# Four or eight of the sixteen d_ff tiles of the input stage as seven products of quarters in blocks 4, 5, 7 and 8, with the attention of those blocks in one PSUM tile and some squares on GpSimd

## The chip, the cores and the metric

The kernel runs on one core of one Trainium2 chip. The metric is device time in microseconds (us) of one execution, from inputs in device memory to the output in device memory; the median of a few executions is given. A profiled execution also has a span, from its first to its last instruction.

## The reference

Attention in chunks of 64 tokens, followed by a feed-forward layer with a squared ReLU:

```python
B, H, S, D = 8, 8, 576, 64            # q, k, v: float32
scores = matmul(q_c, k_c.T) / sqrt(D) # q_c, k_c, v_c: chunks of 64 tokens
attn = softmax(scores)
x = matmul(attn, v_c)                 # -> [B * S, H * D] = [4608, 512]
h = maximum(x @ w_in, 0)              # w_in [512, 2048]
out = (h * h) @ w_out                 # w_out [2048, 512], float32
```

## The kernel before

The 4608 tokens are cut into 18 groups of 256 (`GT`) and the groups, two by two, into nine blocks of 512 tokens, block 0 to block 8 (line 41). Matmuls take bf16 operands and accumulate in float32. d_model = 512 is four row tiles of 128 (`n_dt`), d_ff = 2048 sixteen column tiles (`n_ft`).

**The input stage of a block** is `ffn_in` (line 455). For each of the 16 d_ff tiles `ft`, in `FT_ORDER` 8 to 15 and then 0 to 7, it takes one of four PSUM banks `ps_ffn`, issues four matmuls of 512 columns (line 480: 128 rows of `w_in_bf` stationary, `xT` moving), has ScalarE write the ReLU to `rl` in SBUF (line 471; three buffers), and squares `rl` into `gT`, on VectorE (line 475) or, for tiles 10, 14 and 3, on ScalarE (line 473). From block 3 on `rl` is float32, in blocks 0 to 2 bf16. A `yield` after each tile ends a step, or slot.

**The output stage** is `ffn_out` (line 498; block 0 uses `ffn_out_by_ft`). It multiplies `gT` (512 tokens by 2048) by `w_out` with Winograd's form of Strassen's method: halves of the tokens, of d_ff and of d_model give seven products instead of eight, each 16 matmuls of 256 columns (line 533) in two steps. VectorE makes five differences of quarters of `gT` (line 513, printed as line 493, since the helper `add` records all of them there; `d5`, `d2`, `d1`, `d6`, `d7`, in tiles `w_st`), and combines the products (`w`, `c21`, `s`, `c12`, `c22`, line 493 too). ScalarE copies `n1`, `n2`, `c11` out of PSUM (lines 580, 589, 616).

**Attention runs beside it, one block ahead.** While block j is multiplied, the groups of block j+1 go through `scores` (SC: 32 matmuls into a PSUM tile `ps_att`, exponential on ScalarE, lines 374 and 385), `values` (AV: for each of two token tiles 16 matmuls of 65 columns into a `ps_att` tile, line 401, a reciprocal and a product on VectorE, lines 408 and 409) and `transpose_x` (XT: a DMA transpose from SyncE, line 422, into `xT`). `ps_att` has two buffers of two PSUM banks, so that one tile is filled while another is read. For block j+2 the queries and keys are loaded, cast (CQ, CK; on ScalarE from group 8 on, lines 333 and 340) and transposed by DMA (TD, line 351).

**What sets the order.** The schedule is manual: each engine executes its instructions in the order in which the program issues them. The loop at line 711 writes, for each block, a plan: which of SC, AV, XT, CQ, CK, TD follows which slot (line 745 on: SC after slots 4, AV after 7 and 11, XT after 10 and 14 in blocks 4, 5 and 7 where the line at 750 does not change them), one load per slot in `go_slots`, all on SyncE's queue, and the stores of the block before from slot 20 on (`LATE_STORES`, line 451). The last block has no attention beside it. GpSimd casts the weights and the queries and keys of groups below 8, and issues early and last stores; between 84.7 us and 270.9 us of the span it executes nothing.

## Time and profile before

| | |
|---|---|
| median of three runs | 280.62 us (279.8 to 282.45) |
| the profiled execution: its time | 281.17 us |
| the profiled execution: its span | 279.4 us |
| granted TensorE clock, mean | 0.997 |
| busy: PE, VectorE (DVE), ScalarE (ACT), GpSimd (POOL) | 269.2, 186.5, 160.5, 35.8 us |

The profiled execution's time is 1.8 us above its span and 0.55 us above the median. Times below are us from the start of the span; PE is TensorE's matmuls, PEld its weight loads, and L480 is line 480 of the kernel before. In the groups of instructions a row has the busy time and the mean duration (ns) of one instruction after the count; instructions of one engine overlap a little at their ends, so that a row of them takes less than the sum of their durations. In the chain of waits, pieces of work are listed in order of time, each the one that the next waited for: start, duration, what it was.

The stages of blocks 4 to 8, by the times at which the chain changes from L480 to L533 and back:

| block | input stage with attention | output stage |
|---|---|---|
| 4 | 138.01 to 153.79 | to 166.02 |
| 5 | 166.02 to 181.57 | to 193.80 |
| 6 | 193.80 to 209.61 | to 222.06 |
| 7 | 222.06 to 237.61 | to 249.84 |
| 8 (no attention) | 249.84 to 263.65 | to 275.89 |

### The profile page before, as it was taken

What the parts mean: (1) busy time and instruction counts of PE and PEld (TensorE: products, weight loads), DVE (VectorE), ACT (ScalarE), POOL (GpSimd) and SP (SyncE); (2) the same over time, 40 slices, a digit from 0 to 9 for tenths busy, and PEclk for the clock granted to TensorE, in tenths of its full rate; (3) what the DMA queues carried; (4) which work ended last, traced back from release to release, by engine and by line L of the source; (5) the groups of instructions that cost most, each with busy time, mean ns of one, the idle gap of its engine ahead of it and who ended that gap; (6) DMA issues with size and microseconds to landing.
All of it is one profiled execution on the core that took longest, in us unless ns stands there. A gap on an engine that the chain in (4) does not pass through costs nothing.

```text
span 279.4 us, 7179 instructions
## 1 busy us (share of the span) xinstructions
PE 269.2 (96%) x2960; PEld 176.2 (63%) x2963; DVE 186.5 (67%) x304; ACT 160.5 (57%) x269; POOL 35.8 (13%) x62
## 2 busy tenths in 40 slices
PE   6789999989999999999999999999999999999994
PEld 4544455878774487448744874487448744874584
DVE  1446414998943595579549954995579649955793
ACT  2537615885348862877197719762877197218710
POOL 2037844240171000000000000000000000000012
PEclk9999999999999999999999999999999999999998
DMA  7999999989999999979999999979699964141003
GB/s 236 220 345 358 364 332 240 326 212 194 255 207 244 238 213 191 258 183 198 218 245 260 187 184 298 191 158 185 196 238 208 212 199 40 39 109 44 0 21 131
DMA packets 144384, 57.09 MB, mean 204 GB/s; under 512 B 110624, under 2 KB 141600, under 8 KB 144352
## 3 DMA queue, kind: packets, MB, share of 16 engines
q1 hardware_dynamic: 143296, 53.62, 83.8%
q0 software_dynamic: 912, 2.88, 2.8%
q8 instruction: 23, 0.38, 0.6%
q10 hardware_dynamic: 144, 0.13, 0.1%
q14 instruction: 9, 0.07, 0.1%
HBM read 36.70 MB, written 9.44 MB: 165 GB/s over the span
## 4 chain that ended last, share of the span: by engine, by line
PE 80%; DVE 6%; SPq 4%; ACT 2%; DMA 2%; issue 2%; POOL 0%; DVEq 0%; ACTq 0%
PE ps_ffn L480 39%; PE ps_ffn L533 32%; PE ps_ffn L626 5%; SPq L236 3%; DMA w_st<-in_moe_w_in_dram 2%; DVE x L409 2%; DVE gT L475 2%; DVE w_st L493 2%; ACT rl L471 2%; PE ps_att L401 2%; PE ps_att L374 1%; ACT e L385 1%; SPq L227 1%; PE ps_att L428 1%; PE ps_att L190 1%
## 5 line engine op out<-in xcount | busy, mean ns | idle before, releaser
L480 PE MATMUL ps_ffn<-xT,w_in_bf 128*128 128x512 bf16 (+1 forms) x640 | 130.0, 358 | 0.7 <-POOL w_in_bf L165 0.7
L475 DVE TENSOR_TENSOR gT<-rl 128x512 bf16<-128x512 f32 (+2 forms) x132 | 74.2, 593 | 61.4 <-ACT rl L471 60.7
L471 ACT ACTIVATE rl<-ps_ffn 128x512 f32<-128x512 f32 (+2 forms) x160 | 85.7, 554 | 26.9 <-PE ps_ffn L480 23.3
L480 PEld LDWEIGHTS <-w_in_bf 128*128 128x128 bf16 x640 | 60.5, 98 | 58.2 <-POOL w_in_bf L165 2.2
L533 PEld LDWEIGHTS <-w_st 128*128 128x128 bf16 x640 | 62.0, 98 | 8.2 <-DVE w_st L493 0.9
L493 DVE TENSOR_TENSOR w_st<-gT 128x2048 bf16<-128x2048 bf16 x40 | 47.3, 1217 | 0.2
L533 PE MATMUL ps_ffn<-w_out_bf,w_st 128*128 128x256 bf16 x384 | 45.1, 273 | 0.1
L533 PE MATMUL ps_ffn<-w_sum,w_st 128*128 128x256 bf16 x256 | 29.6, 273 | 0.0
L616 ACT COPY o_sb<-ps_ffn 128x512 f32<-128x512 f32 (+1 forms) x8 | 4.5, 559 | 40.3 <-PE ps_ffn L533 40.3
L533 PEld LDWEIGHTS <-gT 128*128 128x128 bf16 x256 | 24.8, 98 | 4.4 <-DVE gT L475 0.2
L568 POOL DMA_DIRECT2D out_dram<-o_sb x4 | 2.2, 553 | 186.2 <-DVE o_sb L493 186.2
L409 DVE TENSOR_TENSOR x<-ps_att,rec 128x512 bf16<-128x512 f32 x32 | 22.1, 691 | 1.1
L385 ACT ACTIVATE e<-ps_att 128x1024 bf16<-128x1024 f32 x16 | 15.8, 1022 | 4.8 <-PE ps_att L374 4.8
L473 ACT ACTIVATE gT<-rl 128x512 bf16<-128x512 f32 (+2 forms) x28 | 16.8, 599 | 0.9
L533 PE MATMUL ps_ffn<-w_out_bf,gT 128*128 128x256 bf16 x128 | 15.3, 273 | 0.0
L533 PE MATMUL ps_ffn<-w_sum,gT 128*128 128x256 bf16 x128 | 15.3, 273 | 0.0
L626 PE MATMUL ps_ffn<-w_out_bf,gT 128*128 128x512 bf16 x61 | 14.2, 379 | 0.3 <-issue 0.2
L165 POOL CAST w_in_bf<-w_st 128x1024 bf16<-128x1024 f32 (+1 forms) x9 | 9.0, 1001 | 17.9 <-DMA w_st<-in_moe_w_in_dram 17.9
L340 ACT CAST qkb<-k_sb 128x1024 bf16<-128x1024 f32 x10 | 10.5, 1047 | 1.2 <-DMA k_sb<-in_k_dram 1.2
L333 ACT CAST qkb<-q_sb 128x1024 bf16<-128x1024 f32 x10 | 10.4, 1044 | 0.0
L626 PEld LDWEIGHTS <-gT 128*128 128x128 bf16 x64 | 6.0, 98 | 7.0
L401 PEld LDWEIGHTS <-e 64*64 64x64 bf16 x512 | 5.8, 107 | 6.3 <-DVE x L409 2.1
(63 smaller groups left out, 157.1 us busy)
## 6 DMA issues: line engine op xcount, KB each, us to landing
q_sb<-in_q_dram SPq DMA_DIRECT2D x16, 512.0 KB, 6.2
k_sb<-in_k_dram SPq DMA_DIRECT2D x24, 256.0 KB, 5.8
out_dram<-o_sb SPq DMA_DIRECT2D x20, 256.0 KB, 3.7
w_st<-in_moe_w_in_dram SPq DMA_DIRECT2D x8, 512.0 KB, 6.8
w_st<-in_moe_w_out_dram SPq DMA_DIRECT2D x8, 512.0 KB, 6.1
ve_sb<-in_v_dram SPq DMA_DIRECT2D x28, 128.0 KB, 3.5
vo_sb<-in_v_dram SPq DMA_DIRECT2D x21, 128.0 KB, 3.0
out_dram<-o_sb POOLq DMA_DIRECT2D x9, 256.0 KB, 5.5
```

The source lines that it names most:

```text
L333: copy(out=qkb[:, 0].rearrange("p (i h d) -> p i h d", i=2, h=H), in_=qk[g][0].rearrange("p t h d -> p (t h d)").rearrange("p (h i d) -> p ...
L340: copy(out=state["qkb", g][:, 1], in_=qk[g][1].rearrange("p t h d -> p (t h d)"))
L385: nc.scalar.activation(out=e_out, in_=s_in, func=AF.Exp, scale=scale)
L401: nc.tensor.matmul(out=ps[64 * p:64 * p + 64, a, hp * (D + 1):(hp + 1) * (D + 1)], lhsT=e[64 * c:64 * c + 64, a, hp, t, :], rhs=vb[64 * c: ...
L409: nc.vector.tensor_tensor(out=x[:, t].rearrange("p h a d -> p a h d"), in0=o[:, :, :, 0:D], in1=rec.to_broadcast([128, 2, n_hp, D]), op=AL ...
L471: nc.scalar.activation(out=rl[:, 0:n], in_=h[:, 0:n], func=AF.Relu)
L473: nc.scalar.activation(out=gT[:, ft, c:c + n], in_=rl[:, 0:n], func=AF.Square)
L475: nc.vector.tensor_tensor(out=gT[:, ft, c:c + n], in0=rl[:, 0:n], in1=rl[:, 0:n], op=ALU.mult)
L480: nc.tensor.matmul(out=h[:, 0:n], lhsT=w_in_bf[:, dt, ft * 128:(ft + 1) * 128], rhs=xT[:, c // 128:(c + n) // 128, dt, :], start=(dt == 0) ...
L493: engine.tensor_tensor(out=out, in0=in0, in1=in1, op=op)
L533: nc.tensor.matmul(out=outs[t], lhsT=a[:, i, t * 128:(t + 1) * 128], rhs=b[:, i, :], start=(first and i == 0 and (last or t == 0)), stop=( ...
L626: nc.tensor.matmul(out=o_ps[tt], lhsT=gT[:, ft, tt * 128:(tt + 1) * 128], rhs=w_out_bf[:, ft, :], start=(ft == 0), stop=(ft == n_ft - 1))
```

## The change

**Units.** `ffn_in_units` replaces `ffn_in` in blocks 4, 5, 7 (one unit: d_ff tiles 12 to 15) and 8 (two units: 12 to 15 and 4 to 7). A unit computes its four d_ff tiles by seven products instead of eight, with quarters of two d_ff tiles, two d_model tiles and 256 tokens: each product is four matmuls of 256 columns, 28 in all, in place of 16 of 512 columns. A unit has seven steps, `a` (or `b`), placed between the other tiles by `ORDER_U1` and `ORDER_U2`. The products go to the two halves of one `ps_att` tile. A unit has 2 copies (`n1`, `n2`) and a ReLU (`c11`) on ScalarE, on VectorE four combinations with PSUM (`nm`, `c21`, `s`, `c22`) and three fused ReLU-squares (`relu_squared`) from SBUF, on GpSimd one difference (`c12`) and one square. The names `n1`, `nm`, `n2` have one buffer each.

**Weights and tokens.** Five differences of quarters of `w_in` per set of tiles are made on GpSimd: for tiles 12 to 15 issued in block 3, for 4 to 7 in block 7 (slot 20), into query and key buffers. `x_sums`, three VectorE sums or differences of `xT`, are issued before the last product of the output stage of the block before.

**Attention.** In those blocks one `ps_att` tile belongs to the unit and the other serves all of SC and AV, so each scores or values tile writes where the one before was read. The slots are 5, 11, 13, 14 (SC, first AV tile, second AV tile, XT) for the first group and 9, 15, 17, 19 for the second; CQ, CK, TD and the late stores come three slots later.

**Squares.** Of the remaining tiles, 10, 0, 3, 5 are squared on GpSimd, 9, 1, 4 on ScalarE and the rest (8, 11, 2, 6, 7) on VectorE; in block 8, 8, 10, 1, 2 on GpSimd and 9, 11, 0, 3 on ScalarE. `rl` has four buffers instead of three, queries and keys four instead of five.

```diff
--- before.py
+++ after.py
@@ -58,7 +58,7 @@
...
-    in_pool = ctx.enter_context(tc.tile_pool(name="qk", bufs=5))
+    in_pool = ctx.enter_context(tc.tile_pool(name="qk", bufs=4))
...
@@ -74,6 +74,7 @@
...
+    w_dif = w_pool.tile([128, 5, n_dt // 2, 256], BF16, name="w_dif")
...
@@ -363,7 +364,7 @@
...
-        ps = ps_att.tile([128, 1024], FP32, name="ps_att")
+        ps = state.get("ps_att") or ps_att.tile([128, 1024], FP32, name="ps_att")
         for hp in range(n_hp):
             for t in range(2):
                 for a in range(2):
@@ -392,7 +393,8 @@
             state["x", g] = att_pool.tile([128, 2, n_hp, 2, D], BF16, name="x", bufs=3)
         x = state["x", g]
         for t in tiles:
-            ps = ps_att.tile([128, 2, 512], FP32, name="ps_att")
+            ps = state.get("ps_att") or ps_att.tile([128, 1024], FP32, name="ps_att")
+            ps = ps.rearrange("p (a c) -> p a c", a=2)
...
@@ -435,6 +437,12 @@
     C, CQ, CK, TD = cast_qk, cast_q, cast_k, transpose_qk_dma
     SC, AV, XT = scores, values, transpose_x
 
+    def AV0(g):
+        values(g, (0,))
+
+    def AV1(g):
+        values(g, (1,))
+
...
@@ -449,8 +457,144 @@
 
     gTs = {}
     LATE_STORES = {j: 26 if j == 2 else 20 for j in range(2, len(blocks) - 1)}
+    UNITS = {4: (12,), 5: (12,), 7: (12,), 8: (12, 4)}
+    for j in UNITS:
+        if j in LATE_STORES:
+            LATE_STORES[j] += 3
     late = []
     FT_ORDER = [*range(n_ft // 2, n_ft), *range(n_ft // 2)]
+
+    def rl_tile_fp32():
+        return ffn_pool.tile([128, 512], FP32, name="rl", bufs=4)
+
+    difs = {}
+
+    def quarter(f0, i, kk):
+        c = (f0 + 2 * i) * 128
+        return w_in_bf[:, 2 * kk:2 * kk + 2, c:c + 256]
+
+    def w_differences(f0, out):
+        pairs = (((0, 0), (0, 1)), ((1, 1), (1, 0)), ((0, 0), (1, 1)), ((1, 0), (0, 0)),
+                 ((0, 1), (1, 1)))
+        difs[f0] = out
+        for d, (x, y) in zip(out, pairs):
+            add(nc.gpsimd, d, quarter(f0, *x), quarter(f0, *y), ALU.subtract)
+
+    def w_differences_again(_):
+        q_sb = in_pool.tile([128, 2, H, D], FP32, name="q_sb").bitcast(BF16).rearrange(
+            "p t h d -> p (t h d)").rearrange("p (n a f) -> p n a f", n=4, a=2)
+        k_sb = in_pool.tile([128, 2, H, D], FP32, name="k_sb").bitcast(BF16).rearrange(
+            "p t h d -> p (t h d)").rearrange("p (n a f) -> p n a f", n=4, a=2)
+        w_differences(UNITS[8][1], [q_sb[:, n] for n in range(4)] + [k_sb[:, 0]])
+
+    def x_sums(j):
+        xT = xTs[j]
+        st = [wst_pool.tile([128, 1024], FP32, name="w_st").bitcast(BF16) for _ in range(2)]
+        by_dt = st[0][:, 0:1024].rearrange("p (t a q) -> p t a q", t=4, a=2)
+        by_t = st[0][:, 1024:2048].rearrange("p (t a q) -> p t a q", t=2, a=4)
+        cross = st[1][:, 0:512].rearrange("p (t a q) -> p t a q", t=2, a=2)
+        add(nc.vector, by_dt, xT[:, :, 0:2], xT[:, :, 2:4])
+        add(nc.vector, cross, xT[:, 0:2, 0:2], xT[:, 2:4, 2:4], ALU.subtract)
+        add(nc.vector, by_t, xT[:, 0:2], xT[:, 2:4])
+        return by_dt, by_t, cross
+
+    def unit(j, f0, ps):
+        gT, xT = gTs[j], xTs[j]
+        by_dt, by_t, cross = state["x_sums"]
+        n, m = ps[:, 0:512], ps[:, 512:1024]
+        dif = difs[f0]
+
+        def product(out, a, b, first):
+            for f in range(2):
+                for d in range(2):
+                    nc.tensor.matmul(
+                        out=out[:, 256 * f:256 * f + 256],
+                        lhsT=a[:, d, 128 * f:128 * f + 128],
+                        rhs=b[:, :, d, :],
+                        start=(first and f == 0 and d == 0), stop=(d == 1),
+                        skip_group_check=True)
+
+        def kept(name):
+            return ffn_pool.tile([128, 512], FP32, name=name)
+
+        def place_of(i, jj):
+            return gT[:, f0 + 2 * i:f0 + 2 * i + 2, 256 * jj:256 * jj + 256]
+
+        def both(x):
+            return x.rearrange("p (f q) -> p f q", f=2)
+
+        def relu_squared(x, i, jj):
+            nc.vector.scalar_tensor_tensor(
+                out=place_of(i, jj), in0=both(x), scalar=0.0, in1=both(x),
+                op0=ALU.max, op1=ALU.mult)
+
+        product(n, quarter(f0, 1, 1), by_dt[:, 0:2], True)
+        n1 = kept("n1")
+        nc.scalar.copy(out=n1, in_=n)
+        yield
+        product(m, quarter(f0, 0, 0), by_dt[:, 2:4], True)
+        w = kept("nm")
+        add(nc.vector, w, m, n1)
+        yield
+        product(n, dif[0], xT[:, 2:4, 2:4], False)
+        n2 = kept("n2")
+        nc.scalar.copy(out=n2, in_=n)
+        yield
+        product(m, dif[1], xT[:, 0:2, 0:2], False)
+        c21 = rl_tile_fp32()
+        add(nc.vector, c21, w, m, ALU.subtract)
+        c12 = rl_tile_fp32()
+        add(nc.gpsimd, c12, w, n2, ALU.subtract)
+        relu_squared(c21, 1, 0)
+        yield
+        product(n, dif[2], cross, False)
+        s = kept("n1")
+        add(nc.vector, s, n, n2, ALU.subtract)
+        relu_squared(c12, 0, 1)
+        yield
+        product(m, dif[3], by_t[:, :, 0:2], False)
+        c22 = rl_tile_fp32()
+        add(nc.vector, c22, m, s)
+        relu_squared(c22, 1, 1)
+        yield
+        product(n, dif[4], by_t[:, :, 2:4], False)
+        c11 = rl_tile_fp32()
+        nc.scalar.activation(out=c11, in_=n, func=AF.Relu)
+        add(nc.gpsimd, place_of(0, 0), both(c11), both(c11), ALU.mult)
+        yield
+
+    ORDER_U1 = (8, 9, 10, "a", 11, "a", 0, "a", 1, "a", 2, "a", 3, "a", 4, "a", 5, 6, 7)
+    ORDER_U2 = (8, 9, "a", 10, "a", 11, "a", "b", "a", 0, "b", "a", "b", "a", 1, "b", "a", "b",
+                2, "b", "b", 3)
+    SQUARE_BY = {1: {9: "A", 1: "A", 4: "A", 10: "P", 0: "P", 3: "P", 5: "P"},
+                 2: {9: "A", 11: "A", 0: "A", 3: "A", 8: "P", 10: "P", 1: "P", 2: "P"}}
+
+    def ffn_in_units(j):
+        gT, xT = gTs.setdefault(j, ffn_pool.tile([128, n_ft, BT], BF16, name="gT")), xTs[j]
+        ps = [ps_att.tile([128, 1024], FP32, name="ps_att") for _ in range(2)]
+        state["ps_att"] = ps[1]
+        units = UNITS[j]
+        if len(units) == 1:
+            todo, order = {"a": unit(j, units[0], ps[0])}, ORDER_U1
+        else:
+            todo, order = {"a": unit(j, units[0], ps[0]), "b": unit(j, units[1], ps[1])}, ORDER_U2
+        for ft in order:
+            if ft in todo:
+                next(todo[ft])
+                yield
+                continue
+            h = ps_ffn.tile([128, 512], FP32, name="ps_ffn")
+            for dt in range(n_dt):
+                ffn_in_step(h, xT, 0, BT, ft, dt)
+            rl = rl_tile_fp32()
+            nc.scalar.activation(out=rl, in_=h, func=AF.Relu)
+            by = SQUARE_BY[len(units)].get(ft)
+            if by == "A":
+                nc.scalar.activation(out=gT[:, ft], in_=rl, func=AF.Square)
+            else:
+                add(nc.gpsimd if by == "P" else nc.vector, gT[:, ft], rl, rl, ALU.mult)
+            yield
+        state.pop("ps_att")
 
     def ffn_in(j, parts, begun={}):
         if j not in gTs:
@@ -464,10 +608,10 @@
                 ffn_in_step(h, xT, c, n, ft, dt)
             if j < 3:
                 if n == 512 or u % 2 == 0:
-                    rl_tile = ffn_pool.tile([128, 512], FP32, name="rl", bufs=3).bitcast(BF16)
+                    rl_tile = ffn_pool.tile([128, 512], FP32, name="rl", bufs=4).bitcast(BF16)
                 rl = rl_tile[:, u % 2 * 512:] if n < 512 else rl_tile
             else:
-                rl = ffn_pool.tile([128, 512], FP32, name="rl", bufs=3)
+                rl = rl_tile_fp32()
             nc.scalar.activation(out=rl[:, 0:n], in_=h[:, 0:n], func=AF.Relu)
             if (n == 512 and ft in SQUARES_ON_ACT) or (n < 512 and ft in (12, 3)):
                 nc.scalar.activation(out=gT[:, ft, c:c + n], in_=rl[:, 0:n], func=AF.Square)
@@ -609,6 +753,8 @@
         for ps, cols, t in parts("m"):
             add(nc.vector, c22[:, cols], ps, s[:, cols])
             store(nc.gpsimd, c22, 1, HD, t)
+        if j + 1 in UNITS:
+            state["x_sums"] = x_sums(j + 1)
         yield from product("n", d7, b21_p_b22, False)
         c11 = o_tile()
         for ps, cols, t in parts("n"):
@@ -752,18 +898,31 @@
                 loads = itertools.chain(*map(v_pieces, nxt), loads)
                 slots = {SC: (8, 10), AV: (12, 15), XT: (15, 18), C: (20, 23), TD: (22, 25)}
                 go_slots = [*range(16), *range(25, 36)]
+            late_by = 0
+            if j in UNITS:
+                late_by = 3
+                go_slots = range(35)
+                for i, g in enumerate(nxt):
+                    for slot, f in zip(((5, 11, 13, 14), (9, 15, 17, 19))[i], (SC, AV0, AV1, XT)):
+                        at(slot, f, g)
+                nxt = []
+            if j == 3:
+                at(2, lambda _: w_differences(UNITS[4][0], [w_dif[:, n] for n in range(5)]), None)
+            if j == 7:
+                at(20, w_differences_again, None)
             for f in (SC, AV, XT):
                 for i, g in enumerate(nxt):
                     at(slots[f][i], f, g)
             if j > 2 and far and is_whole(far[0]):
                 for slot, f, i in ((16, CQ, 0), (18, CK, 0), (18, TD, 0), (18, CQ, 1),
                                    (19, CK, 1), (19, TD, 1)):
-                    at(slot, f, far[i])
+                    at(slot + late_by, f, far[i])
             else:
                 for f in (C, TD):
                     for i, g in enumerate(far):
-                        at(slots[f][i], f, g)
-            phases = [ffn_in(j, [(0, BT, FT_ORDER)]), ffn_out(j)]
+                        at(slots[f][i] + late_by, f, g)
+            phases = [ffn_in_units(j) if j in UNITS else ffn_in(j, [(0, BT, FT_ORDER)]),
+                      ffn_out(j)]
         slot = 0
         for phase in phases:
             for _ in phase:
```

## Prediction

> **What bounds the kernel now.** I read the page's busy shares first, then the chain of waits in order of time, then the groups of instructions by shape, and last the timelines of VectorE, ScalarE and GpSimd inside block 4. TensorE is the bound, and not only in the mean:
>
> ```profile
> PE 269.2 (96%) x2960; PEld 176.2 (63%) x2963; DVE 186.5 (67%) x304; ACT 160.5 (57%) x269; POOL 35.8 (13%) x62
> ```
>
> The chain of waits shows where. From block 4 on it runs on PE almost without a break:
>
> ```profile
> 138.01 4.32 PE ps_ffn L480 x20
> 142.33 0.38 PE ps_att L374 x32
> ...
> 146.28 3.56 PE ps_ffn L480 x16
> 149.84 0.39 PE ps_att L401 x27
> 150.23 3.56 PE ps_ffn L480 x16
> 153.79 12.23 PE ps_ffn L533 x112
> ...
> 249.84 13.81 PE ps_ffn L480 x64
> 263.65 12.24 PE ps_ffn L533 x112
> ```
>
> The last two lines give the two prices that count: 13.81 / 64 = 0.2158 us for a matmul of 512 columns, 12.23 / 112 = 0.1092 for one of 256. The groups by shape give the other engines' prices:
>
> ```profile
> L475 DVE TENSOR_TENSOR gT<-rl 128x512 bf16<-128x512 f32 x78 | 51.2, 687 | 41.6 <-ACT rl L471 41.1
> L409 DVE TENSOR_TENSOR x<-ps_att,rec 128x512 bf16<-128x512 f32 x32 | 22.1, 691 | 1.1
> L385 ACT ACTIVATE e<-ps_att 128x1024 bf16<-128x1024 f32 x16 | 15.8, 1022 | 4.8 <-PE ps_att L374 4.8
> L165 POOL CAST w_in_bf<-w_st 128x512 bf16<-128x512 f32 x2 | 1.2, 613 | 14.7 <-DMA w_st<-in_moe_w_in_dram 14.7
> ```
>
> Back to back, VectorE's instructions of 512 follow each other by 0.605 (two in 1.29), ScalarE's ReLUs by 0.50, its exponentials by 0.92; a dependent square starts 0.63 after its ReLU. ScalarE starts 0.25 after a tile's last matmul slot (tile begun 137.85, ReLU at 138.97). VectorE or ScalarE releases PE in 0.04 to 0.05.
>
> The timelines hold one more fact, from block 0, the only stretch with the weight casts: a VectorE square, 0.42 alone, takes 1.07 when it starts inside a GpSimd cast, and ends just after it.
>
> ```profile
> 23.46 0.42 DVE L475 TENSOR_TENSOR gT<-rl 128x512 bf16<-128x512 bf16 x1 [1.49 <-ACT rl L471]
> 25.25 1.07 DVE L475 TENSOR_TENSOR gT<-rl 128x512 bf16<-128x512 bf16 x1 [0.19 <-ACT rl L471]
> 25.00 1.04 POOL L165 CAST w_in_bf<-w_st 128x1024 bf16<-128x1024 f32 x1 [0.22 <-DMA w_st<-in_moe_w_in_dram]
> ```
>
> It goes the other way too: a cast at 78.75 took 1.31 because a float32 sum of two SBUF tiles was on VectorE. Products with a PSUM operand beside casts (74.16) kept their 0.69. So two-SBUF-input work on VectorE and work on GpSimd exclude each other.
>
> **The saving.** A unit replaces 16 x 0.2158 = 3.45 by 28 x 0.1092 = 3.06: 0.39 us. Five units: 2.0 us, all on PE, the bound. The 256-column price comes from 112 matmuls that each load weights, as these will.
>
> **The cost in a block with attention.** I follow the queues from the block's first matmul at 0. PE: a tile 0.863, a product 0.437, SC 0.32, an AV tile 0.195. Work alone is 48 x 0.2158 + 28 x 0.1092 + 0.64 + 0.78 = 14.84 (before 15.23).
>
> First wait. AV's first tile overwrites the scores of group 2, so it needs their exponential. ScalarE gets ReLU 1 at 7.07, its square at 7.70, the exponential at 8.23, done 9.25. PE is there at 8.87 and starts at 9.30: 0.4 lost.
>
> Second wait. AV's second tile overwrites the first, so it needs VectorE's product x. ReLU 2 stands behind that exponential (9.15 to 9.75); VectorE then has, in this order, square 2 (9.78), s (10.39), the fused ReLU-square of c12 (10.99), the reciprocal (11.60) and x (11.83 to 12.52). PE, after tile 3 and a product, is there at 10.77 and starts at 12.55: 1.8 lost.
>
> Third wait. VectorE goes on with c22 (12.43), its ReLU-square (13.14), reciprocal (13.75), x (13.98 to 14.67). The second group's first AV tile could start at 14.04 and starts at 14.71: 0.65 lost. Its second tile finds x done (16.06 against 16.62).
>
> The stage ends at 14.84 + 2.84 = 17.68. The output stage after it does not wait: VectorE's first difference is done at 21.0, PE asks for it at 21.2. Before, the stages of blocks 4, 5 and 7 took 15.78, 15.55 and 15.55 against 15.23 of work; I cannot place that 0.3 and keep it: 17.98, hence 2.2 + 2.4 + 2.4 = 7.0 us longer. The fused ReLU-square is in no row: 0.69 as the square of the same size, at most the 1.22 of VectorE's longest two-input row; I take 0.69, and 1.22 would add up to 1 per block.
>
> **GpSimd's price.** A two-input operation of 512 is in no row. It lies between the one-input cast of 512 (0.61) and two casts of 1024 (2.1); I take 1.04, the cast of 1024, which reads as many elements. In blocks 4 and 5 this costs nothing more: square 0 ends at 7.5, c12 at 8.6, long before 10.99; ReLU-square c21 waits 0.2 for c12, in time that VectorE would idle. The Trainium skill ("GPSIMD Engine Reference", "Performance versus the Vector engine") calls GpSimd the wrong engine for ordinary elementwise work: 4497 ns for a two-input add of 2048, so by estimate 1.1 for 512; no run here shows it. By the page the sum below would grow by about 1 us.
>
> **Block 7's output stage.** The five differences of w_in stand behind square 5 in GpSimd's queue and wait for nothing else that is late, so they run from 17.7 on, against VectorE's last squares and its differences d5, d2, d1, d6. Taking turns, d5 ends at 21.7 instead of 21.0, d2 at 23.6, d6 at 27.5; PE waits 0.5, 0.8 and 0.4: 1.7 us.
>
> **Block 8.** Work alone is 32 x 0.2158 + 56 x 0.1092 = 13.02, against 13.81. But the units share one nm: the second unit's sum waits for c12 of the first on GpSimd (6.35 to 7.40), the ReLU-squares wait for GpSimd (0.7, then 0.9 behind square 1), and VectorE's fourteen instructions then stand almost without a gap: c21 of the second unit ends at 12.6 where PE asks at 11.3, s at 14.0 where PE asks at 13.1. Waits 1.35 + 0.95, end 15.37: 1.6 us longer.
>
> **Costed at nothing.** x_sums (about 1.7 us, by 0.69 or less for 1024 and 0.43 for 512) lie in the 2.61 us that VectorE idles before a block's first square; they need xT. SyncE issued the second transpose at 161.5 (landing 3.4 later) behind its loads; the change puts all loads before both transposes, and x_sums then come at about 167: 1 to 2 us to spare. If not, the first square and the unit's first product stand behind them. The first set of w_in differences waits for nothing and runs at 85 to 90 us, when GpSimd is idle and VectorE has gaps of 1 to 3 us. Casts, transposes for block j+2 and stores, three slots later, fall into the output stage, where ScalarE is busy 5.5 of 12.2 us. Four buffers for queries and keys are enough: what is loaded in one block is read two blocks later. A fourth rl buffer can give back at most the 2.1 us in which ReLUs waited for VectorE, off PE's path.
>
> **Sum.** 7.0 + 1.7 + 1.6 = 10.3, the saving already inside. 281.17 + 10.3 = 291.5 for the profiled execution; it lay 0.55 above the median, so 290.9: about 291.
>
> **Rivals.** (1) GpSimd does not matter: its operations take 0.61, or nothing is excluded. The three attention waits stay (no GpSimd result is the last to arrive), block 7's tail costs 0 to 0.7, block 8 0 to 0.9: 281.17 + 7.0 + 0.8 - 0.55 = about 288. For it: float32 sums on VectorE were not slowed at 78.48. Against: the 1.07. (2) GpSimd is slow: at 1.5 us square 0 and c12 reach past 9 and push the ReLU-square of c21 and all behind it; the same walk gives 2.8 + 3.0 + 7.1 + 3.8 = 16.7, about 298. For it: two inputs never seen. (3) Faster: PE does not wait for attention, because VectorE reaches x in time. Then the 2.0 us remain: 281.17 - 2.0 - 0.55 = about 279. It decides if the waits of a block stay under 0.39, the unit's saving. Against: even with ReLU 2 at once, square, s, ReLU-square, reciprocal and x need 2.7 us where tile 3 and a product give 1.3. (4) The change does not do what it says, if products of four matmuls pay more per matmul than the output stage's: excluded up to the 0.1092 row.
>
> **How the numbers follow.** The walk as above 0.6, (1) 0.17, (2) 0.13, (3) 0.1. The low end, 285, is (1) with each block's waits 0.6 shorter; the high end, 297, is a GpSimd price of 1.4 (14.6 by the same walk, plus the kept 0.9). About 1% (2.8 us) is what a measurement of this kernel can tell from no change: faster 0.06, same 0.06, slower 0.88.
>
> **What would show it.** In the profile after: PE idle at the AV line, released by VectorE's x, about 1.8 and 0.65 us per block in blocks 4, 5, 7; input stages near 18 us; GpSimd rows of 1.04 us; d5 and d2 of block 7 at about 2 us each; block 8's input stage near 15.4. I am wrong if the AV line shows no such idle time, or if GpSimd's rows are far from 1.04.

## The result and the profile after

The changed kernel takes 298.31 us (median of six, 297.32 to 300.02) beside 281.09 for the kernel before (six, 279.8 to 282.7): ratio 1.061, 95% interval 1.056 to 1.066. It is slower, as forecast, but by 17.2 us instead of 10, and outside the range of 285 to 297. The profiled execution took 298.99 us, with a span of 297.2.

The page's busy shares of the changed kernel:

```profile
PE 274.3 (92%) x3020; PEld 183.6 (62%) x3023; DVE 201.8 (68%) x314; ACT 158.0 (53%) x265; POOL 82.3 (28%) x98
```

PE's share fell from 96% to 92%: PE waits. It is also recorded as busy for 5.1 us more, although its work became less. 2.1 us of that lie in block 8, mostly from a slower clock (see below); 2.7 lie in blocks 4 to 7, where the granted clock was 1.00, and were not traced further. Where PE waits is read from the times at which it changes between d_ff tiles and output products (us; "own tiles" is the first experiment):

| stage | before | forecast | after | own tiles |
|---|---|---|---|---|
| block 4, 5, 7 input | 15.78, 15.55, 15.55 | 17.98 | 18.52, 18.53, 18.54 | 18.10, 18.10, 18.09 |
| block 7 output | 12.23 | 13.9 | 14.50 | 14.51 |
| block 8 input | 13.81 | 15.4 | 20.26 | 14.87 |
| block 8 output, to its last product | 12.40 | 12.4 | 12.76 | 13.35 |

Blocks 4, 5 and 7 and the tail of block 7 are within 0.6 of the forecast each (in part by luck, see below). Block 8 lost 6.8 us where 1.6 was forecast. PE's timeline in block 8 of the changed kernel (start, duration; in brackets the idle time before it and who ended it; L510 is a unit's product, L624 a d_ff tile):

```profile
264.56 0.60 PE L510 MATMUL ps_att<-w_st,w_in_bf 128*128 128x256 bf16 x4 [0.58 <-ACT n L533]
...
267.85 0.60 PE L510 MATMUL ps_att<-xT,w_dif 128*128 128x256 bf16 x4 [0.80 <-ACT n L541]
...
270.65 0.60 PE L510 MATMUL ps_att<-xT,q_sb 128*128 128x256 bf16 x4 [0.47 <-DVE nm L637]
271.44 0.60 PE L510 MATMUL ps_att<-w_st,w_dif 128*128 128x256 bf16 x4 [0.20 <-DVE n L637]
...
274.19 0.60 PE L510 MATMUL ps_att<-w_st,q_sb 128*128 128x256 bf16 x4 [0.41 <-DVE rl L637]
...
275.86 0.60 PE L510 MATMUL ps_att<-w_st,q_sb 128*128 128x256 bf16 x4 [0.21 <-DVE n L637]
278.53 1.01 PE L510 MATMUL ps_att<-w_st,k_sb 128*128 128x256 bf16 x4 [2.08 <-DVE rl L637]
279.34 1.91 PE L624 MATMUL ps_ffn<-xT,w_in_bf 128*128 128x512 bf16 x4
```

The first line shows what the forecast had missed. It is a unit's second product. It writes the half `m`, which nobody has read yet, but it waits for ScalarE's copy of the other half, `n` (L533). The two halves are slices of one `ps_att` tile. The reading, tested by the first experiment, is that the program's waits are set by tile: each product waits for the reader of the product directly before it, not of the one two before.

The last two lines show something else: four matmuls of 512 columns take 1.91 instead of 1.03. The granted clock, by stretches (from:to, length, busy time of PE, PEld, DVE, ACT, POOL with counts, clock, DMA share, GB/s), is 0.50 there. In all it stays at 0.50 for 3.4 us, from 278.4 to 281.8:

```profile
276.30:278.50 2.20, 0.15 (x2) 0.00 (x0) 2.11 (x2) 0.04 (x1) 2.20 (x3) 0.97 0.00 0
278.50:279.34 0.84, 0.81 (x5) 0.54 (x4) 0.81 (x1) 0.00 (x0) 0.28 (x1) 0.50 0.00 0
279.34:281.05 1.71, 1.71 (x6) 0.59 (x5) 0.00 (x0) 0.60 (x1) 0.75 (x1) 0.50 0.00 0
```

In block 4, PE waits at the AV line for VectorE's x, as forecast, but for less:

```profile
151.24 0.22 PE L403 MATMUL ps_att<-ve_sb,e 64*64 64x65 bf16 x2 [0.84 <-DVE x L411]
...
153.40 0.22 PE L403 MATMUL ps_att<-ve_sb,e 64*64 64x65 bf16 x2 [0.43 <-DVE x L411]
```

What the forecast said of the other engines came out. GpSimd's rows by shape, and the fused ReLU-square, in the changed kernel:

```profile
L637 POOL TENSOR_TENSOR gT<-rl 128x512 bf16<-128x512 f32 x21 | 22.7, 1084 | 149.6 <-ACT rl L590 138.5 <-ACT rl L562 11.0
L637 POOL TENSOR_TENSOR q_sb<-w_in_bf 128x512 bf16<-128x512 bf16 x4 | 7.3, 1865 | 0.0
L637 POOL TENSOR_TENSOR rl<-nm,n 128x512 f32<-128x512 f32 x5 | 6.8, 1365 | 1.7 <-ACT n L541 1.7
L527 DVE SCALAR_TENSOR_TENSOR gT<-rl 128x512 bf16<-128x512 f32 x15 | 12.2, 813 | 0.9 <-POOL rl L637 0.6
```

GpSimd's squares of 512 take 1.04 in the median (1.08 in the mean), the value taken. The difference `c12` takes 1.27 at least, the differences of `w_in` 1.14 to 2.13. VectorE's fused operation, 0.69 in the median, takes up to 1.51. In block 7's output stage both are slowed side by side: `d5` and `d2` take 2.04 each there (before the change 1.2), as forecast.

```profile
248.39 4.08 DVE L637 TENSOR_TENSOR w_st<-gT 128x2048 bf16<-128x2048 bf16 x2
246.13 7.35 POOL L637 TENSOR_TENSOR q_sb<-w_in_bf 128x512 bf16<-128x512 bf16 x4
```

So the two do hold each other up.

### The profile page after: what moved, and what is told of

Same layout as the page of the kernel before. It is cut to its first block, busy times and chain, and to the rows that moved or that the text cites. A ratio compares the mean times of both kernels' runs of the same rounds, so it can differ in the third digit from the quotient of the medians.

```text
span 297.2 us, 7344 instructions
## 1 busy us (share of the span) xinstructions
PE 274.3 (92%) x3020; PEld 183.6 (62%) x3023; DVE 201.8 (68%) x314; ACT 158.0 (53%) x265; POOL 82.3 (28%) x98
## 5 line engine op out<-in xcount | busy, mean ns | idle before, releaser
L624 PE MATMUL ps_ffn<-xT,w_in_bf 128*128 128x512 bf16 (+1 forms) x560 | 117.0, 357 | 0.9 <-POOL w_in_bf L166 0.9
L624 PEld LDWEIGHTS <-w_in_bf 128*128 128x128 bf16 x560 | 52.2, 98 | 45.0 <-POOL w_in_bf L166 2.4
L619 DVE TENSOR_TENSOR gT<-rl 128x256 bf16<-128x256 bf16 (+2 forms) x80 | 44.6, 594 | 30.2 <-ACT rl L615 29.7
L637 POOL TENSOR_TENSOR gT<-rl 128x512 bf16<-128x512 f32 x21 | 22.7, 1084 | 149.6 <-ACT rl L590 138.5
L615 ACT ACTIVATE rl<-ps_ffn 128x512 bf16<-128x512 f32 (+2 forms) x96 | 48.3, 526 | 16.1 <-PE ps_ffn L624 14.6
L590 ACT ACTIVATE rl<-ps_ffn 128x512 f32<-128x512 f32 x44 | 26.3, 597 | 23.6 <-PE ps_ffn L624 23.6
L677 PEld LDWEIGHTS <-gT 128*128 128x128 bf16 x256 | 25.1, 99 | 4.8 <-issue 0.6
L637 DVE TENSOR_TENSOR gT<-rl 128x512 bf16<-128x512 f32 x15 | 10.9, 728 | 16.5 <-ACT rl L590 16.5
L527 DVE SCALAR_TENSOR_TENSOR gT<-rl 128x512 bf16<-128x512 f32 x15 | 12.2, 813 | 0.9 <-POOL rl L637 0.6
L510 PEld LDWEIGHTS <-w_dif 128*128 128x128 bf16 x80 | 7.8, 97 | 8.1 <-issue 4.6
```

What stands on the lines that cost most here:

```text
L510: nc.tensor.matmul(out=out[:, 256 * f:256 * f + 256], lhsT=a[:, d, 128 * f:128 * f + 128], rhs=b[:, :, d, :], start=(first and f == 0 and ...
L527: nc.vector.scalar_tensor_tensor(out=place_of(i, jj), in0=both(x), scalar=0.0, in1=both(x), op0=ALU.max, op1=ALU.mult)
L590: nc.scalar.activation(out=rl, in_=h, func=AF.Relu)
L615: nc.scalar.activation(out=rl[:, 0:n], in_=h[:, 0:n], func=AF.Relu)
L619: nc.vector.tensor_tensor(out=gT[:, ft, c:c + n], in0=rl[:, 0:n], in1=rl[:, 0:n], op=ALU.mult)
L624: nc.tensor.matmul(out=h[:, 0:n], lhsT=w_in_bf[:, dt, ft * 128:(ft + 1) * 128], rhs=xT[:, c // 128:(c + n) // 128, dt, :], start=(dt == 0) ...
```

## Experiments

Ratios are to the kernel before, with their 95% intervals. Stage times are from the profiled execution of each kernel.

### One tile or two: what block 8 lost

**Own tiles.** `ps_att` is closed at a unit block and opened again as `ps_unit`, with one-bank tiles, in the same PSUM banks (excerpt):

```diff
-        n, m = ps[:, 0:512], ps[:, 512:1024]
+        n, m = ps
...
-        ps = [ps_att.tile([128, 1024], FP32, name="ps_att") for _ in range(2)]
-        state["ps_att"] = ps[1]
+        ps = [[ps_unit.tile([128, 512], FP32, name=f"ps_{c}{i}") for c in "nm"]
+              for i in range(len(UNITS[j]))]
+        if len(UNITS[j]) == 1:
+            state["ps_att"] = ps_unit.tile([128, 1024], FP32, name="ps_att")
```

> Edit: in the unit blocks the two halves n and m of a unit's PSUM tile become two tiles of one bank each; same instructions, same order, same GpSimd work. Theory (a product waits for the reader of the product directly before it, because both lie in one tile): each product then waits for the reader two products before; the input stage of block 8 goes from 20.26 to 15.5 to 16.0 us, without the idle time of 2 us before the last product and with the clock kept; the input stages of blocks 4, 5 and 7 go from 18.5 to 17.9; block 7's output stage stays at 14.5. In all 298.3 - 6.3 = about 292. Rival 1 (VectorE and GpSimd exclude each other and are simply full in block 8): block 8 stays above 19 us, total 297 to 298.3. Rival 2 (the tiles matter, but only in block 8): blocks 4, 5, 7 stay at 18.5, total about 294.

Measured: 293.29 us, ratio 1.042 (1.038 to 1.047). Block 8's input stage falls from 20.26 to 14.87, more than expected, and those of 4, 5, 7 by 0.43 each, less than the 0.6 expected. Block 8's output stage rose from 12.76 to 13.35, which was not expected. Both rivals fall. With own tiles block 8 stands 2.0 us (both stages) above the kernel before; the forecast, which had taken the halves as independent, said 1.6. The waits left in block 8 are fewer and late (last line: the second output product, L680, waits for a square):

```profile
272.00 0.60 PE L511 MATMUL ps_m<-w_st,q_sb 128*128 128x256 bf16 x4 [0.37 <-DVE rl L640]
273.45 0.60 PE L511 MATMUL ps_n<-w_st,k_sb 128*128 128x256 bf16 x4 [0.85 <-DVE n L640]
...
277.72 1.53 PE L680 MATMUL ps_ffn<-w_out_bf,gT 128*128 128x256 bf16 x12 [0.74 <-ACT gT L596]
```

**The clock.** `keep_busy(20)`, matmuls on constant data, after the second unit's sixth product fills the gap of 2.2 us; its results are not used.

> Edit: 20 matmuls of 256 columns on constant data, about 2.2 us at full clock, go into block 8 between the second unit's sixth and seventh product, where PE is idle for 2.2 us; nothing else changes. Theory (the idle time lowers the clock, and the slow matmuls after it are a price of their own): the granted clock stays near 1 until the end, the tile of four matmuls after the gap takes 0.86 instead of 1.71, the first product of the output stage 1.75 instead of 2.11; block 8 in all 1.5 to 2 us shorter, total about 296.5. Rival (the slow matmuls after the gap have another cause, such as operands that arrive late): those durations stay, total 298.3 or more, since the added matmuls fill the gap at best.

Measured: 297.52 us, 1.059 (1.055 to 1.062), 1 us above the expected total; in the profile the input stage of block 8 takes 19.03 and its output stage 12.39, together 1.6 us less than in the changed kernel, and the tile after the gap takes its full-clock 1.03:

```profile
277.46 2.35 PE L327 MATMUL ps_ffn<-ident_f,ident 128*128 128x256 bf16 x20
279.71 0.60 PE L510 MATMUL ps_att<-w_st,k_sb 128*128 128x256 bf16 x4
280.14 1.03 PE L629 MATMUL ps_ffn<-xT,w_in_bf 128*128 128x512 bf16 x4
```

The 1.6 us are the clock's, but not in every execution. Three kernels further down have the same unfilled gap (idle 2.08). The one with earlier differences kept a clock of 1.00 in its profile, and its block 8 took the same 19.03 and 12.39 without anything in the gap; the two with gated differences and one tile for a unit fell to 0.50. This fits a median that moved by only 0.8. The Trainium skill ("TensorE: Matmul & The Clock Gate", "What's actually happening") has the clock fall to half after an idle window of about 3.4 us; here an idle time of 2.1 was enough, in three of the four profiles that have it. An idle time of 1.9 (the moved differences with 64 bytes, below) did not lower it.

**No GpSimd arithmetic in the unit blocks.**

```diff
-        add(nc.gpsimd, c12, w, n2, ALU.subtract)
         relu_squared(c21, 1, 0)
+        c12 = rl_tile_fp32()
+        add(nc.vector, c12, w, n2, ALU.subtract)
...
-        add(nc.gpsimd, place_of(0, 0), both(c11), both(c11), ALU.mult)
+        nc.scalar.activation(out=place_of(0, 0), in_=both(c11), func=AF.Square)
```

> Edit, to the changed kernel: in the unit blocks GpSimd does no arithmetic any more. In blocks 4, 5, 7 its squares of tiles 10 and 3 go to ScalarE and of 0 and 5 to VectorE, in block 8 those of 1 and 2 to ScalarE and of 8 and 10 to VectorE; c12 goes to VectorE (behind the ReLU-square of c21) and the square of c11 to ScalarE. The units' halves stay in one PSUM tile, the w_in differences where they are. Theory (the products wait for the reader of the product before, and attention for its one tile; GpSimd is not what they wait for): by the walk of the queues the input stages of 4, 5, 7 become 0.3 to 0.7 us longer, since VectorE has more to do, and block 8's changes by less than 0.7 but for the clock; total 297.5 to 300.5. Rival (the turns that GpSimd and VectorE take are what block 8 lost): block 8's input stage falls from 20.26 to 16 or less, total 294 or less.

Measured: 297.71 us, 1.059 (1.055 to 1.063). Stages of 19.11 in blocks 4, 5, 7 (0.6 longer) and 18.79 in block 8, against 19.03 with GpSimd at full clock. GpSimd's arithmetic is not what block 8 lost to. With nothing else in GpSimd's queue, the second set of differences ran in block 5's output stage, from 192.9 on, and that stage took 12.81; block 7's fell to 12.23.

**No units in block 8.** `UNITS` without 8, no second set of differences.

> Edit: block 8 has no units (its input stage is that of the kernel before), and the second set of w_in differences is gone; blocks 4, 5 and 7 are as in the changed kernel. Theory (the parts add up): input stages of 4, 5, 7 at 18.5, block 7's output stage 12.25, block 8's input stage 13.8, output 12.24; total 281.1 + 3 x 2.9 + 0.2 = 290.0. Rival (block 7's unit itself makes the tail late, or what block 7 leaves late makes block 8 late): block 7's output stage above 13, or block 8's input stage above 14.5, total above 291.

Measured: 290.21 us, 1.033 (1.029 to 1.037); 18.5 three times, block 7's output stage 12.22, block 8 as before the change. The total was the 290.0 expected: the parts add up.

### The attention in one tile

**Spread slots**, on the kernel with own tiles: `((2, 8, 11, 12), (5, 14, 17, 18))` for `((5, 11, 13, 14), (9, 15, 17, 19))`.

> Edit, to the kernel of e1 (own tiles for n and m): the attention of blocks 4, 5, 7 is spread over the stage: SC after slots 2 and 5, the four AV tiles after 8, 11, 14, 17, the transposes after 12 and 18 (instead of SC 5 and 9, AV 11, 13, 15, 17). One PSUM tile for attention as before, all else as in e1. Theory (each AV tile waits for the reader of the tile before it, and two slots are too short for that): the waits at the AV line nearly vanish, and the input stages go from 18.10 to 16.2 to 16.6 (the walk gives 16.0 without the 0.3 that no walk places); total 293.3 - 3 x 1.7 = about 288.2. Rival (the one tile costs its time wherever the slots lie, since VectorE's x comes late): the stages stay above 17.5, total above 291.5.

Measured: 289.14 us, 1.027 (1.022 to 1.031); 16.67, 16.63, 16.61, so about 1.5 less per block. Of the waits at the AV line (1.53 and 0.43 in block 4 with own tiles, first line) one is left (second line):

```profile
151.20 0.22 PE L404 MATMUL ps_att<-ve_sb,e 64*64 64x65 bf16 x2 [1.53 <-DVE x L412]
```

```profile
149.87 0.22 PE L404 MATMUL ps_att<-ve_sb,e 64*64 64x65 bf16 x2 [0.76 <-DVE x L412]
```

**All waits out**: own tiles, no GpSimd arithmetic, attention still earlier, products at other places (the order is in the expectation).

> Edit: e1's own tiles and e7's gated differences together with a new order: in blocks 4, 5, 7 tile 8, products 1 and 2, tile 9, products 3 and 4, tiles 10, 11, 0, product 5, tiles 1, 2, product 6, tile 3, product 7, tiles 4 to 7; SC after slots 1 and 4, AV after 8, 11, 14, 17; in block 8 the order of the two units follows the same idea; no GpSimd arithmetic in these blocks (squares of 11, 0, 1, 2, 7 on ScalarE, in block 8 of 9, 10, 11, 0, 2, 3; the rest, c12 too, on VectorE; the square of c11 on ScalarE). Theory (the units' saving of 0.39 us each is real, and only waits hide it): by the walk the input stages of 4, 5, 7 take 15.0 to 15.6 (15.55 to 15.78 before the change), block 8's 13.0 to 13.6 (13.8 before); total 279 to 281 beside 281.1. Rival (units cost more than they save whatever the order, by VectorE's and ScalarE's added work): stages above 16.2 and 14.2, total above 283.

Measured: 290.31 us, 1.031 (1.027 to 1.035). The expected 279 to 281 was missed. Block 8's input stage took 13.02, exactly the work alone. Block 5's took 15.83, but block 4's 21.02 and block 7's 17.69, since the scores now asked for queries and keys that were still being transposed:

```profile
148.00 0.44 PE L377 MATMUL ps_att<-qkT 64*64 64x64 bf16 x32 [3.06 <-DMA qkT<-qkb]
```

**Later scores** take that away.

> Edit, to e8: the scores of blocks 4, 5, 7 come after slots 5 and 8 instead of 1 and 4 (AV after 11, 13, 16, 18), since in e8 PE waited 0.3 and 3.1 us in block 4 and 1.8 in block 7 for transposed queries and keys that were still on SyncE's queue; product 4 is followed by tile 10, product 5, tiles 11, 0, 1, 2, product 6, tiles 3, 4, 5, product 7, tiles 6, 7; squares of 1, 3, 7, 2 on ScalarE; w_in differences and buffers as in e9. Theory (that wait was all that was left of e8's loss): no wait for these transposes, input stages of blocks 4, 5, 7 at 15.0 to 15.7, of block 8 at 13.0, total 279.0 to 280.5. Rival (in a block with attention VectorE and ScalarE have no room for a unit without GpSimd): stages of 16 or more, total above 282.

Measured: 287.91 us, 1.016 (1.011 to 1.021), far above the theory's 279.0 to 280.5, with stages of 15.95, 15.82, 16.23, 13.02 and time lost elsewhere: block 3's input stage took 17.27 instead of 15.56 (see below). In blocks 4 and 5 no wait of PE is listed any more, in block 7 0.9 for transposes. So even nearly without waits a unit block with attention is no shorter than before.

**Attention split, no units**, in the kernel before:

```diff
+            if j in (4, 5, 7):
+                for i, g in enumerate(nxt):
+                    for slot, f in zip(((4, 7, 8, 10), (5, 11, 12, 14))[i], (SC, AV0, AV1, XT)):
+                        at(slot, f, g)
+                nxt = []
```

> Edit, to the kernel before, no units at all: in blocks 4, 5 and 7 the attention stands in six places of the input stage instead of three (SC after slots 4 and 5 instead of both after 4, the AV tiles after 7, 8, 11, 12 instead of two after 7 and two after 11); two PSUM tiles, all squares and buffers as before. Theory (each separate turn from d_ff tiles to attention and back costs PE about 0.2 us: in the kernel before a pair of SC takes 0.73 from the end of one d_ff tile to the start of the next, in e10 a single one 0.46; a pair of AV tiles 0.50, in e6 a single one 0.36): input stages 0.6 longer, 16.2 to 16.4, total about 281.1 + 1.9 = 283. Rival (the single ones are longer for another reason, such as the units beside them): stages within 0.15 of 15.78, 15.55, 15.55, total 281.

Measured: 283.95 us, 1.008 (1.005 to 1.011), stages of 16.23 in all three (0.45, 0.68, 0.68 longer). The theory holds; here is why, PE before (one pair of SC, 64 matmuls) and with the split (two single ones):

```profile
170.27 0.71 PE L374 MATMUL ps_att<-qkT 64*64 64x64 bf16 x64
170.91 0.82 PE L480 MATMUL ps_ffn<-xT,w_in_bf 128*128 128x512 bf16 x3
```

```profile
171.98 0.45 PE L374 MATMUL ps_att<-qkT 64*64 64x64 bf16 x32
172.35 1.04 PE L486 MATMUL ps_ffn<-xT,w_in_bf 128*128 128x512 bf16 x4
173.32 0.45 PE L374 MATMUL ps_att<-qkT 64*64 64x64 bf16 x32
173.70 0.39 PE L486 MATMUL ps_ffn<-xT,w_in_bf 128*128 128x512 bf16 x1
```

From SC's start to the next tile a pair takes 0.64, two single ones 0.37 + 0.38, and each turn adds some 0.1 of idle time before it. With one `ps_att` tile the attention stands in six turns instead of three: 0.45 to 0.68 us per block, more than the 0.39 that a unit saves.

### The differences of w_in

**Earlier issue**: `w_differences_again` after slot 2 of block 6.

> Edit: the second set of five w_in differences on GpSimd is issued after slot 2 of block 6 instead of slot 20 of block 7. Theory (GpSimd and VectorE take turns, and in block 7's output stage VectorE has no time to give): that stage goes from 14.50 to 12.25 us, block 6's input stage stays within 0.4 of 15.88, total 296.0 to 296.5. Rival 1 (their price only moves): block 6's input stage grows by 1 to 2 us, total 297.5 to 298.3. Rival 2 (block 7's tail is late for other reasons, such as its own unit's last squares and x_sums): the stage stays above 14, total 298.

Measured: 298.76 us, 1.062 (1.057 to 1.067). Block 7's output stage fell to 12.23, but block 5's rose to 14.51. GpSimd's queue was empty and nothing made the instructions wait, so they ran long before the slot they were issued at, right behind block 5's last squares (input stage's end at 186.9):

```profile
184.69 2.12 POOL L637 TENSOR_TENSOR gT<-rl 128x512 bf16<-128x512 f32 x2 [3.15 <-ACT rl L562]
186.78 7.36 POOL L637 TENSOR_TENSOR q_sb<-w_in_bf 128x512 bf16<-128x512 bf16 x4
```

The price moved almost to the hundredth: 2.27 in block 7, 2.28 in block 5. An output stage has little VectorE time to give (in block 7's before the change VectorE is busy for 11.0 of 12.25 us). But the place within the stage counts: without GpSimd arithmetic (above) the same five began 3.6 us into block 5's output stage and cost 0.58 there.

**Behind a gate** in block 3:

```diff
+                at(2, lambda _: (
+                    nc.gpsimd.tensor_copy(out=gate[:, 0:1], in_=gTs[3][:, FT_ORDER[0], 0:1]),
+                    w_differences(UNITS[8][1], [w_dif[:, n] for n in range(5, 10)])), None)
```

> Edit, to the changed kernel: the second set of w_in differences is made in block 3, behind a GpSimd copy of one column that waits for block 3's first square, so that GpSimd cannot run ahead to it; it has a tile of its own (for its space the exponentials and the attention outputs have two buffers instead of three). Theory (what matters is what VectorE has to do while GpSimd runs: in block 3's input stage it is busy less than half of the time, in an output stage it is not to spare): block 7's output stage 12.2, no other stage longer by more than 0.3; total 296. Rival (five differences cost about 2.3 us wherever they run): block 3's input stage or the output stage after it grows by 1.5 us or more.

Measured: 297.56 us, 1.059 (1.054 to 1.063). Block 7's output stage 12.22 and block 3's input stage unchanged (15.56), so five differences cost nothing there, although VectorE was busy for 59% of that stage before the change and not for less than half. But block 2's input stage took 17.75 instead of 15.85. Neither theory had a place for that.

### Time lost where nothing was changed

The first kernels with the gate (gated differences and all waits out among them) all lost time outside the unit blocks.

> Edit, to e8: units in block 8 only, with e8's order of their products (its input stage took 13.02 us in e8 against 13.82 before); blocks 4 to 7 as in the kernel before. Seven of the ten w_in differences on GpSimd in block 3 behind the gate, the last three on VectorE behind x_sums, at the start of block 8; the exponentials and attention outputs have three buffers again. Theory (the units' saving is 0.39 us each and nothing else is lost): input stages of blocks 4 to 7 as before the change, block 8's 13.0, output stage 12.4; total 280.3, 0.8 below before, by about the measurement's own uncertainty. Rival (the extra work costs elsewhere, in block 3 or in block 7's output stage, where 14 vector instructions stand): some stage longer by 1 us or more, total 281.5 or above.

Measured: 287.32 us, 1.019 (1.015 to 1.023): the rival came true. Block 8's input stage took 13.02, but block 3's took 17.27 instead of 15.56, with seven differences beside it (PE waited 1.4 for VectorE's x), and block 6's output stage 13.98 instead of 12.45, behind a key load that came late. So five differences cost nothing in block 3 and seven cost 1.7.

> Edit, to e9 (units in block 8 only): the two sets of five w_in differences are made on GpSimd in the input stages of blocks 6 and 7, each behind a copy of one column that waits for that block's first square, into query and key buffers that are free by then; so there are five buffers for queries and keys and three for rl again, as in the kernel before, and no tile for differences; in block 8 products and squares have an order worked out for three rl buffers. Theory (in e7 five differences in an input stage cost 0.2 us in all, in e9 seven cost 1.7, and e9's late keys came from its four buffers): input stages of blocks 6 and 7 and their output stages within 0.5 of before, block 8's input stage 13.0 to 13.6, blocks 2 to 5 as before; total 280 to 281.5. Rival (five differences cost about 2 us in these stages too, where VectorE has more to do than in block 3): blocks 6 and 7 together 3 us or more longer, total above 283.5.

Measured: 287.74 us, 1.020 (1.015 to 1.024), blocks 3, 4 and 6 late in the same way (output stages of 13.53, 13.08 and 14.20), in 3 and 4 long before the first difference is made. What the late kernels share is the gate: a tile of 4 bytes among the constants, which takes 32, so that all tiles behind it lie 32 bytes further.

**The shift alone**, in the kernel before:

```diff
+    gap = const_pool.tile([128, 2], BF16, name="gap")
+    nc.gpsimd.memset(gap, 0.0)
```

> Edit, to the kernel before, no units: one tile of 4 bytes per partition more among the constants (set to zero once by GpSimd, never read). It takes 32 bytes, so that all tiles that are loaded, cast and transposed begin 32 bytes after a multiple of 64 instead of on one; the gate of e7 to e11 did the same. Theory (those kernels lost 3 to 6 us outside the unit blocks by this shift): the DMA packets' time, 234 us per engine before (83.8% of the span of 279.4), rises to 240 to 245, queries and keys land later, total 284 to 287. Rival (the shift does nothing; e9 and e11 lost their time by the differences and the buffers): packets' time 230 to 237, total 281.

Measured: 286.70 us, 1.017 (1.012 to 1.022), as the theory expected.

> Edit, to the kernel before: as e13, but the added tile takes 64 bytes. If multiples of 64 bytes are all that counts, total 281 to 282; if multiples of 128 count (e14 had its tiles 64 past one, and still lost 3.4 us in block 6's output stage and the input stage before it, with packets at 238.7 us), total 283.5 to 286.5.

Measured: 287.82 us, 1.019 (1.014 to 1.023), above both expected ranges.

> Edit, to the kernel before: as e13, but the added tile takes 256 bytes per partition (only the first 4 are set), so that all later tiles keep their place with respect to multiples of 256 bytes. Theory (e13's loss is the place of the tiles in their 64 or 128 bytes): total 281 to 282, packets' time 230 to 237 us. Rival (the added tile or its memset costs, wherever the tiles lie): total 285 or above.

Measured: 281.10 us, 0.997 (0.994 to 1.000). So not the added tile costs, but where it pushes the others. Chosen waits with the shift of 32 (engine, line, releaser: us in total, times, longest) and with 256:

```profile
ACT qkb L342 <- DMA k_sb<-in_k_dram: 3.9, 4, 1.3
ACT qkb L335 <- DMA q_sb<-in_q_dram: 2.2, 2, 1.5
PE ps_att L376 <- DMA qkT<-qkb: 2.1, 5, 0.5
PE ps_ffn L535 <- ACT n L591: 1.9, 2, 1.1
PE ps_ffn L482 <- DMA xT<-x: 1.3, 2, 0.7
```

```profile
ACT qkb L342 <- DMA k_sb<-in_k_dram: 1.1, 3, 0.6
PE ps_att L376 <- DMA qkT<-qkb: 0.4, 1, 0.4
```

Keys land late, ScalarE's cast waits for them, the copy `n2` stands behind the cast, and PE waits for `n2`. In block 6's output stage with the shift of 32:

```profile
219.14 1.04 ACT L342 CAST qkb<-k_sb 128x1024 bf16<-128x1024 f32 x1 [0.94 <-DMA k_sb<-in_k_dram]
220.09 0.58 ACT L591 COPY n<-ps_ffn 128x512 f32<-128x512 f32 x1
```

The rise of the packets' time was small (240.3 us per engine with 32 and 242.3 with 64, against 234.1 before and 237.4 with 256), so it doesn't by itself explain the delay. The Trainium skill ("DMA: Bandwidth & Descriptors", "How a descriptor splits into AXI transactions") has a transaction start only at a multiple of 256 bytes, with bytes fetched for nothing otherwise. In the kernel before, half of the tiles, the weights among them, lie at 128 past such a multiple. Whether this rule is the cause, no run shows; the runs say only that 32 and 64 more cost and 256 more do not. The changed kernel is not touched by this: its one new tile, `w_dif`, takes 5120 bytes, a multiple of 256.

**The moved differences again, with 64 and 256 bytes.**

> Edit, to e11: the gate takes 64 bytes per partition instead of 32, so that all tiles lie on multiples of 64 bytes as in the kernel before. Theory (shift): blocks 2 to 5 as in the kernel before, block 6's and block 7's input stages 15.8 to 16.2 and their output stages 12.2 to 12.8, block 8's input stage 13.0; packets' time back to 230 to 237; total 280 to 282. Rival (e11 lost its time by the five differences in blocks 6 and 7 and by units as such): total above 285.

Measured: 287.57 us, 1.020 (1.015 to 1.025), block 6's output stage 15.04. So 64 bytes do not give the time back, as the shift of 64 alone showed above.

> Edit, to e7 (the changed kernel with the second set of differences in block 3 behind the gate): the gate takes 64 bytes instead of 32. Theory (shift; five differences cost little in block 3's input stage): block 2's input stage back from 17.75 to 15.9, the output stage of block 7 at 12.2, total 294.5 to 296.5. Rival (what e7 lost in block 2 came from two buffers instead of three for exponentials and attention outputs): block 2's input stage stays above 17, total 297.5.

Measured: 299.47 us, 1.062 (1.055 to 1.068), block 2's input stage 16.44, between the two expectations; what the two buffers cost there was not separated.

> Edit, to e11: the gate takes 256 bytes, so that all tiles keep their place with respect to 256 bytes. Theory: block 6's output stage 12.3 to 12.9 instead of 14.2 and 15.0, its input stage and block 7's 15.8 to 16.2, block 8's input stage 13.0; total 280 to 282, with the units' 0.8 of block 8 and up to 0.9 lost again to the two sets of differences. Rival (block 6's output stage was late by the differences made before it): it stays above 13.8, total 284 or above.

Measured: 282.30 us, 1.002 (0.999 to 1.005), so no different from before. The rival falls. Its stages show the whole balance: block 8's input 13.02 (0.79 less), block 6's 16.06 and block 7's 16.13 (0.25 and 0.58 more beside the differences; PE waits 0.3 for ScalarE's exponential in the one and 0.4 for VectorE's x in the other), output stages as before. The units' saving is real, and making their differences costs all of it.

## Why the prediction was wrong

- **What bounds, and the attention waits: right in kind.** PE is the bound and waits at the AV line for VectorE's x: 0.84 and 0.43 in block 4 and, once the products no longer wait, 1.53 and 0.43, where 1.8 and 0.65 were forecast (the first wait, forecast at 0.4, is too short to be listed). Spreading the slots takes most of it away.
- **That blocks 4, 5 and 7 came so close is partly luck.** With own tiles the stage of block 4 is 18.10, 3.26 above the 14.84 of work. The listed waits make 1.96 of it, 0.9 less than the 2.84 forecast; the rest is 1.30, 1.0 more than the 0.3 kept. The two errors nearly cancel.
- **"I cannot place that 0.3": placed.** It is the attention's turns on PE, which the walk had costed at SC 0.32 and AV 0.195 without the change-over. Kept at 0.3, they are 0.45 to 0.68 more in a unit block, by the split attention.
- **GpSimd's price: right for the squares** (1.04), low for the differences (1.14 to 2.13); that the two engines hold each other up is right. Block 7's tail was mis-sized: 2.27 where 1.7 was forecast. Its three listed waits are 0.49, 0.77 and 0.53, against 0.5, 0.8 and 0.4. But an idle time is listed from the modelled end of the matmul before. From start to start (1.74 for an unhindered sixteen) the same waits cost 0.66, 0.95 and 0.70, which is the whole 2.3.
- **Failed: the walk of block 8, "Waits 1.35 + 0.95", 1.6 us longer.** Its waits came from the shared `nm`, from GpSimd and from VectorE's queue; in PSUM it let each product start when the reader of its own half was done. The program makes it wait for the reader of the product before, whichever half. With two units woven together PE meets that wait again and again: 3.2 us in block 8 (31.42 for both stages with one tile and full clock, 28.22 with own tiles), and 0.43 in each of blocks 4, 5 and 7, 1.3 together. With own tiles the two waits of the walk are there, shorter (0.37 for `c21`, 0.85 for `s`), and a third that it did not have (0.74 for a square on ScalarE): 2.0 us in all, against 1.6.
- **Missed: the clock.** The last of the waits for one tile, 2.1 us, could lower the clock: 1.6 us in the profiled execution. So block 8's 6.8 are 3.2 for the tile, 1.6 for the clock and 2.0 that own tiles leave.
- **Rival 2 had the number, 298, but not the cause.** It needed GpSimd operations of 1.5 us; the squares took 1.04, and without GpSimd's arithmetic the kernel took 297.71.
- **Right: the 0.39 saved per unit** (block 8's input stage at 13.02 against 13.81 in six kernels), `x_sums` at nothing (they end the output stages of blocks 3, 4 and 6, which took 12.50, 12.22 and 12.26, before 12.56, 12.23 and 12.45), the first set of differences at nothing in block 2 (15.85 against 15.79).

Sum for the profile: 8.7 in blocks 4, 5, 7, 2.3 in block 7's tail and 6.8 in block 8 make the 17.8 by which the span grew; the other differences cancel. Of the 7 us beyond the forecast own tiles give back 5 in the medians.

## What to carry to other kernels

Ask of each buffer at which grain its waits are set: here two halves of one tile that alternate were one buffer, and the chain on it ran at the pace of its readers, not of the matmuls. Weigh a saving on the bound engine against what it costs on the others: 0.39 us per unit did not pay for five differences on an engine that holds up a busy one, nor for three more turns of the attention. An instruction on an idle queue runs as soon as its data and its buffer are ready, not at the slot where it is written. A new small tile ahead of the others moves all of them: padding it to 256 bytes cost nothing here.

## What the runs showed of the hardware that was not expected

- All SBUF tiles 32 or 64 bytes further: ratios of 1.017 (1.012 to 1.022) and 1.019 (1.014 to 1.023); 256 bytes further: 0.997 (0.994 to 1.000). By which transfer it begins was not settled.
- An idle time of 2.1 us on PE lowered the granted clock to 0.50 for 3.4 us, in three of four profiled executions.
- Single groups of small matmuls between large ones come with some 0.1 us of idle time on PE before each; six turns instead of three cost 0.45 to 0.68 us a block.
- Five differences on GpSimd cost PE 0 to 2.3 us, by the stage and the place in it: nothing in block 3's input stage, 0.25 and 0.58 in those of blocks 6 and 7, 0.58 or 2.28 in block 5's output stage. Seven in block 3's input stage cost 1.7.
